# The two fp32 head loads of k, issued by SyncE and ScalarE at once, in an attention and FFN kernel bound by TensorE

## Chip, cores, metric

The kernel runs on one core of a Trainium2 chip. The metric is the device time of one execution in microseconds (us). The "span" of a profile runs from the first to the last instruction of the program; the time is some 1.8 us longer than the span.

## The reference

Cross-covariance attention (channels attend to channels) in four batches, then a maxout FFN with three up-projections.

```python
# q, k, v: (4, 6144, 256) float32
qn = q / (norm(q, axis=1) + 1e-6);  kn = k / (norm(k, axis=1) + 1e-6)
s  = kn.transpose(0, 2, 1) @ qn / tau            # (4, 256, 256)
a  = softmax(s, axis=-1)
x  = (v @ a).reshape(4 * 6144, 256)
h  = maximum(maximum(x @ w1, x @ w2), x @ w3)    # d_ff = 768
out = h @ w_out
```

## The kernel before

Before any FFN work can start, the whole of q and k of batch 0 must be read and their Gram matrix formed. POOL loads both with a cast from float32 to fp8 on the way (the software queue). Only the first 8 of k's 48 row groups, the "head", come as float32 through SyncE's hardware queue, in two halves, and are cast on VectorE and ScalarE, so that TensorE can start early.

```python
HEAD = 8
kf = consts.tile([P, HEAD, C], FP32, name="kf")
HH = HEAD // 2
for i in range(2):
    SP.dma_start(out=kf[:, i * HH:(i + 1) * HH, :], in_=k_r[0][:, i * HH:(i + 1) * HH, :])
for load, widths in ((load_k, [8] * 5), (load_q, [8] * 5 + [4, 2, 2])):   # POOL, fp32 -> fp8
    ...
DVE.tensor_copy(out=qk[0][1][:, 0:HH, :], in_=kf[:, 0:HH, :], saturate=False)
ACT.activation(out=qk[0][1][:, HH:HEAD, :], in_=kf[:, HH:HEAD, :], func=AF.Copy, saturate=False)
...
def gram(b):
    for tp in range(NG // 2):          # 24 pairs of row groups: squares of k, 2 matmuls each
        ... PE.matmul(kk[:, jsl], lhsT=kt[:, tsl, jsl], rhs=kt[:, tsl, jsl], ...)
    ... dkm = kk * ident               # VectorE
    for tp in range(NG // 2):          # 24 pairs: q against k, and squares of q, 4 matmuls each
        ... PE.matmul(ps[j][:, 0:C], lhsT=qt[:, tsl, jsl], rhs=kt[:, tsl, :], ...)
        ... PE.matmul(ps[j][:, C:C + P], lhsT=qt[:, tsl, jsl], rhs=qt[:, tsl, jsl], ...)
```

The q loads have widths 8, 8, 8, 8, 8, 4, 2, 2, so the fifth full load feeds pairs 16 to 19 of the second loop and the last small one feeds pair 23 alone.

Of the kernel before, what the change touches and what calls it, by code (L numbers as in the profile page):

```python
# [31 lines left out]
def kernel(  # L32
# [15 lines left out]
    ACT = nc.scalar  # L48
    POOL = nc.gpsimd
    SP = nc.sync  # L50
# [15 lines left out]
    k_r = k.rearrange("b (p g) c -> b p g c", p=P)  # L66
# [48 lines left out]
    HEAD = 8  # L115
    kf = consts.tile([P, HEAD, C], FP32, name="kf")
    HH = HEAD // 2
    for i in range(2):
        SP.dma_start(out=kf[:, i * HH:(i + 1) * HH, :], in_=k_r[0][:, i * HH:(i + 1) * HH, :])
    for load, widths in ((load_k, [8] * 5), (load_q, [8] * 5 + [4, 2, 2])):  # L120
        g0 = HEAD if load is load_k else 0
        for w in widths:
# [358 lines left out]
```

## Time and profile before

| | kernel before |
|---|---|
| time, median of the first 3 runs | 576.76 us |
| span of the profile | 574.9 us |
| kf halves have landed (their casts start) | 4.68 and 5.93 us |
| fifth full q load lands | 31.27 us |
| last q load lands | 33.44 us (18.43 us issue + 15.0 us) |

The page's list of DMA issues shows what is loaded in the head: columns are destination and source, issuing queue, count, KB each (as written), and the median us from issue to landing.

```profile
k_sb<-in_k_dram POOLq DMA_DIRECT2D x5, 256.0 KB, 10.8
q_sb<-in_q_dram POOLq DMA_DIRECT2D x5, 256.0 KB, 19.4
kf<-in_k_dram SPq DMA_DIRECT2D x2, 512.0 KB, 4.3
```

A time to landing of 10 or 19 us for 256 KB says that these loads stand in a queue. The issue is early, the DMA engines are the limit.

### The profile page before, as it was taken

How to read it: one execution, taken by the hardware profiler on the slowest of the kernel's cores; microseconds unless marked ns; L12 is line 12 of the kernel's file. 1: busy time of each engine (PE TensorE's matmuls, PEld its weight loads, DVE VectorE, ACT ScalarE, POOL GpSimd, SP SyncE). 2: the span in 40 equal slices, each digit the busy share in tenths (PEclk: the TensorE clock that was granted, in tenths of full speed). 3: DMA queues.
4: the chain of work that ended last, by engine and by line, in shares of the span. 5: the costliest groups of instructions: out<-in, count | busy, mean ns of one | idle time of the engine just before them, and what ended most of it. 6: DMA issues, size and time to landing. Idle time of an engine off the chain costs nothing.

```text
span 574.9 us, 9325 instructions
## 1 busy us (share of the span) xinstructions
PE 555.1 (97%) x3328; PEld 328.5 (57%) x3328; DVE 406.4 (71%) x627; ACT 307.2 (53%) x530; POOL 227.3 (40%) x235
## 2 busy tenths in 40 slices
PE   3789999999999999999999999999999999999996
PEld 3655555555755555555575555555575555555554
DVE  0048777777577777777748777777848778778774
ACT  1034567677454466776735447767646444444442
POOL 4232257776731028777761006777760000000000
PEclk9999999999999999999999999999999999999999
DMA  9998998885598228977378526788535234322111
GB/s 142 107 144 157 130 178 124 157 133 113 102 118 164 59 66 155 133 152 130 75 131 130 114 75 101 157 131 130 125 84 127 66 82 129 74 91 76 56 73 74
DMA packets 75951, 65.62 MB, mean 114 GB/s; under 512 B 52353, under 2 KB 61953, under 8 KB 75905
## 3 DMA queue, kind: packets, MB, share of 16 engines
q0 software_dynamic: 18928, 26.48, 39.1%
q1 hardware_dynamic: 56832, 38.28, 22.9%
q8 instruction: 26, 0.43, 0.3%
q10 hardware_dynamic: 144, 0.26, 0.1%
q14 instruction: 21, 0.16, 0.1%
HBM read 78.64 MB, written 25.17 MB: 181 GB/s over the span
## 4 chain that ended last, share of the span: by engine, by line
PE 93%; DMA 5%; ACT 0%; DVE 0%; issue 0%; POOL 0%; DVEq 0%; POOLq 0%
PE h_ps L327 65%; PE o_ps L346 21%; DMA q_sb<-in_q_dram 4%; PE gram L235 3%; PE ew_ps L282 3%; DMA k_sb<-in_k_dram 2%; PE o_ps L366 0%; PE gram L178 0%; PE n_ps L216 0%; PE n_ps L218 0%; ACT et L246 0%; PE gram L180 0%; DVE o_sb L372 0%; POOL k_sb L99 0%; DVE scr L253 0%
## 5 line engine op out<-in xcount | busy, mean ns | idle before, releaser
L327 PE MATMUL h_ps<-vt_sb,aw_sb 128*128 128x512 bf16 x1728 | 406.6, 379 | 0.0
L331 DVE TENSOR_TENSOR s_mx<-h_ps,s_mx 128x512 bf16<-128x512 f32 x288 | 197.9, 687 | 98.1 <-ACT s_mx L330 97.1
L327 PEld LDWEIGHTS <-aw_sb 128*128 128x128 bf16 x1728 | 168.2, 98 | 163.0 <-DVE aw_sb L288 3.7
L330 ACT ACTIVATE s_mx<-h_ps 128x512 bf16<-128x512 f32 x288 | 171.4, 595 | 130.7 <-PE h_ps L327 130.7
L332 DVE TENSOR_TENSOR ht_sb<-h_ps,s_mx 128x512 bf16<-128x512 f32 x288 | 199.2, 692 | 30.7 <-PE o_ps L346 0.5
L204 POOL TENSOR_TENSOR acc<-acc,sq 128x768 f32<-128x768 f32 x90 | 147.7, 1651 | 70.7 <-ACT sq L198 70.5
L346 PE MATMUL o_ps<-wo_sb,ht_sb 128*128 128x256 bf16 x1128 | 153.9, 273 | 0.0
L346 PEld LDWEIGHTS <-ht_sb 128*128 128x128 bf16 x1128 | 110.4, 98 | 52.9
L349 ACT ACTIVATE o_sb<-o_ps 128x512 f32<-128x512 f32 x94 | 56.1, 597 | 83.1 <-PE o_ps L346 83.1
L110 POOL DMA_DIRECT2D v_sb<-in_v_dram x48 | 26.8, 562 | 88.5 <-DMA vt_sb<-v_sb 86.6
L198 ACT ACTIVATE sq<-q_sb 128x768 bf16<-128x768 fp8e4 x48 | 40.5, 844 | 0.0
L198 ACT ACTIVATE sq<-k_sb 128x768 bf16<-128x768 fp8e4 x48 | 40.1, 835 | 0.0
L201 POOL CAST acc<-sq 128x768 f32<-128x768 bf16 x6 | 4.9, 821 | 64.6 <-ACT sq L198 64.6
L102 POOL DMA_DIRECT2D q_sb<-in_q_dram x32 | 17.7, 555 | 10.7 <-DMA k_sb<-in_k_dram 9.7
L166 PE MATMUL kk<-k_sb 128*128 128x256 fp8e4 x48 | 7.8, 339 | 11.7 <-DVE k_sb L152 5.4
L285 ACT ACTIVATE aw_sb<-ew_ps,rinv 128x384 bf16<-128x384 f32 (+1 forms) x27 | 14.4, 546 | 5.7 <-PE ew_ps L282 4.8
L282 PE MATMUL ew_ps<-w_sb,et 128*128 128x384 bf16 (+1 forms) x108 | 17.1, 308 | 0.0
L235 PE MATMUL gram<-k_sb,q_sb 128*128 128x512 fp8e4 x144 | 16.8, 277 | 0.0
L99 POOL DMA_DIRECT2D k_sb<-in_k_dram x29 | 16.0, 554 | 1.0 <-POOLq L462 0.8
L235 PEld LDWEIGHTS <-q_sb 128*128 128x256 fp8e4 x144 | 15.9, 136 | 0.6
L178 PE MATMUL gram<-k_sb,q_sb 128*128 128x512 fp8e4 x48 | 10.7, 323 | 3.4 <-DMA q_sb<-in_q_dram 3.4
L166 PEld LDWEIGHTS <-k_sb 128*128 128x256 fp8e4 x48 | 6.5, 182 | 12.8 <-DMA k_sb<-in_k_dram 6.3
(52 smaller groups left out, 103.6 us busy)
## 6 DMA issues: line engine op xcount, KB each, us to landing
out_dram<-o_sb SPq DMA_DIRECT2D x47, 512.0 KB, 2.8
v_sb<-in_v_dram POOLq DMA_DIRECT2D x48, 256.0 KB, 3.7
k_sb<-in_k_dram POOLq DMA_DIRECT2D x24, 192.0 KB, 5.3
q_sb<-in_q_dram POOLq DMA_DIRECT2D x24, 192.0 KB, 6.8
k_sb<-in_k_dram POOLq DMA_DIRECT2D x5, 256.0 KB, 10.8
q_sb<-in_q_dram POOLq DMA_DIRECT2D x5, 256.0 KB, 19.4
w_sb<-in_moe_w_dram POOLq DMA_DIRECT2D x9, 128.0 KB, 5.7
kf<-in_k_dram SPq DMA_DIRECT2D x2, 512.0 KB, 4.3
```

The lines of the kernel that those rows point to most:

```text
L102: POOL.dma_start(out=qk[b][0][:, g0:g0 + w, :], in_=q_r[b][:, g0:g0 + w, :])
L110: POOL.dma_start(out=t, in_=v_r[gi // NCH, gi % NCH])
L198: ACT.activation(out=sq, in_=src, func=AF.Square)
L204: POOL.tensor_tensor(out=acc, in0=acc, in1=sq, op=ALU.add)
L235: PE.matmul(g[:, j * C:(j + 1) * C], lhsT=qt[:, tsl, j * P:(j + 1) * P], rhs=kt[:, tsl, :], start=(tp == 0 and j == 0), stop=(tp == NG // ...
L282: PE.matmul(ew[:, :w], lhsT=et[:, j, ic * P:(ic + 1) * P], rhs=w_sb[m][:, j, fsl], start=(j == 0), stop=(j == CC - 1))
L327: PE.matmul(t.rearrange("p (t n) -> p t n", t=TPC), lhsT=aw[m][:, ic, fsl], rhs=vt[:, :, ic, :], start=(ic == 0), stop=(ic == CC - 1))
L330: ACT.activation(out=s_mx, in_=hp[0], func=AF.Copy)
L331: DVE.tensor_tensor(out=s_mx, in0=hp[1], in1=s_mx, op=ALU.max)
L332: DVE.tensor_tensor(out=ht[:, fc, :], in0=hp[2], in1=s_mx, op=ALU.max)
L346: PE.matmul(st["ps"][:, half], lhsT=ht[:, fc, t * P:(t + 1) * P], rhs=wo_sb[:, fc, :], start=(fc == 0), stop=(fc == FC - 1))
L349: ACT.activation(out=st["o"][:, t - 1:t + 1, :].rearrange("p t d -> p (t d)"), in_=st["ps"], func=AF.Copy)
```

## The change

The intent: SyncE needs 0.4 us to issue each half, so the second half is issued late. With ScalarE issuing the second one, both start together.

```diff
-    for i in range(2):
-        SP.dma_start(out=kf[:, i * HH:(i + 1) * HH, :], in_=k_r[0][:, i * HH:(i + 1) * HH, :])
+    for i, eng in enumerate((SP, ACT)):
+        eng.dma_start(out=kf[:, i * HH:(i + 1) * HH, :], in_=k_r[0][:, i * HH:(i + 1) * HH, :])
```

## The prediction

> **What bounds the kernel now.** I read the page first, for the balance of the engines and the chain that ended last, and then the first 60 us of the chain in order of time, because the diff touches only the first 6 us.
>
> ```profile
> span 574.9 us, 9325 instructions
> PE 555.1 (97%) x3328; PEld 328.5 (57%) x3328; DVE 406.4 (71%) x627; ACT 307.2 (53%) x530; POOL 227.3 (40%) x235
> ...
> PE 93%; DMA 5%; ACT 0%; DVE 0%; issue 0%; POOL 0%; DVEq 0%; POOLq 0%
> ```
>
> The reader is to see that TensorE carries 93% of the chain and DMA 5%. A head load can touch only that 5%, which is 29 us. The chain in order of time says which 29 us:
>
> ```profile
> 1.23 0.67 POOL k_sb L99
> 1.90 8.89 DMA k_sb<-in_k_dram
> 10.79 0.28 issue
> 11.07 20.20 DMA q_sb<-in_q_dram
> 31.27 0.04 issue
> 31.32 0.32 PE gram L178
> ```
>
> Start, duration, piece. The chain goes through the software-queue loads (those that POOL issues, float32 to fp8) until 31.27 us, and from there through TensorE to the end. The two kf loads and the two casts out of kf are not in it by name. So the time of this kernel is, to a good approximation, "when the last q load lands" plus 543.6 us of TensorE work that the change does not touch. The question is whether the kf loads decide when the last q load lands. For that I read the instructions of the first 8 us in order of time:
>
> ```profile
> 0.73 1.28 ACT L144 ACT_TABLE_LOAD   x1 [0.73 <-PEq L462]
> 0.74 0.87 SPq L119 DMA_DIRECT2D kf<-in_k_dram  x2
> 1.23 2.79 POOL L99 DMA_DIRECT2D k_sb<-in_k_dram  x5 [0.78 <-POOLq L462]
> 4.68 0.69 DVE L152 CAST k_sb<-kf 128x1024 fp8e4<-128x1024 f32 x1 [3.40 <-DMA kf<-in_k_dram]
> 5.93 1.06 ACT L153 ACTIVATE k_sb<-kf 128x1024 fp8e4<-128x1024 f32 x1 [3.91 <-DMA kf<-in_k_dram]
> 8.35 1.07 PEld L166 LDWEIGHTS <-k_sb 128*128 128x256 fp8e4 x8 [0.75 <-DMA k_sb<-in_k_dram]
> 8.35 1.25 PE L166 MATMUL kk<-k_sb 128*128 128x256 fp8e4 x8 [0.57 <-DMA k_sb<-in_k_dram]
> ```
>
> SyncE issues both kf loads in 0.87 us, the second at about 1.15 us. The halves land at 4.68 and 5.93 us. TensorE has done both halves by 7.8 us and then waits for the first software load at 8.35 us. Last, the stretches, with the columns window, length, busy time of PE, PEld, DVE, ACT and POOL, granted clock, DMA share, GB/s:
>
> ```profile
> 1.50:2.00 0.50, 0.00 (x0) 0.00 (x0) 0.00 (x0) 0.50 (x1) 0.50 (x2) 1.00 0.78 106
> 2.00:2.50 0.50, 0.00 (x0) 0.00 (x0) 0.00 (x0) 0.02 (x1) 0.50 (x2) 1.00 0.73 123
> 2.50:3.00 0.50, 0.00 (x0) 0.00 (x0) 0.00 (x0) 0.00 (x0) 0.50 (x2) 1.00 0.81 213
> 3.50:4.00 0.50, 0.00 (x0) 0.00 (x0) 0.00 (x0) 0.00 (x0) 0.50 (x2) 1.00 1.07 434
> 12.00:14.00 2.00, 0.82 (x7) 0.74 (x6) 0.00 (x0) 0.00 (x0) 0.49 (x1) 1.00 1.07 108
> ```
>
> The DMA engines are busy from 1.75 us (first packet of kf in the packet records) without a gap. The rate is counted in bytes written, so the 108 GB/s of the fp8 stage reads four times as much, 432 GB/s, the same as the 434 of the kf stage at its best. The one weak stretch is 1.75 to 3.0 us, where the engines are "busy" at 0.73 to 0.81 but move only 106 to 213 GB/s: the first packets take 0.2 to 1.2 us each instead of the 0.159 us of the later ones. Two queue rows (packets, MB, share), up to 3.00 us and up to 4.75 us, finish the picture:
>
> ```profile
> q1 hardware_dynamic: 54, 0.22, 38.8%
> ...
> q1 hardware_dynamic: 243, 0.93, 60.8%
> q0 software_dynamic: 1, 0.00, 0.4%
> ```
>
> The software queue (q0), whose first load was issued by 1.90 us, moves its first packet only at 4.74 us, when kf (q1) is nearly drained. In the packet records each DMA engine starts its first software packet some 6 ns after its own last kf packet, between 4.74 and 5.5 us. So kf holds the software loads back, and through them it is on the path after all: whatever makes kf drain sooner moves the last q load and the whole span by the same amount.
>
> **What the skill says.** The Trainium skill, page "DMA: Bandwidth & Descriptors", section "Issuing engines are not separate DMA queues", says that loads started from several engines run on the same 16 DMA engines and that doing so "will only save the time on the sequencer it takes to initiate the DMA". Here that time is about 0.4 us (0.87 us for two issues). The same page, section "Where 436 GB/s comes from", puts the ceiling of the fabric at 435 GB/s; this trace agrees with 432 to 434, so there is no spare rate for a second issuer. Its section "Queues, rings and completion order" has each DMA engine go round its queues packet by packet. The trace of before does not look like that between the hardware and the software queue (no software packet before 4.74 us), so I don't count on fair sharing. The page "ScalarE: Activation LUTs", section "What ACT_TABLE_LOAD costs", gives a load of 1283 ns; the trace shows 1.28 us.
>
> **The change part by part.** The comparison of instruction streams shows one DMA issue leaving SyncE and one arriving on ScalarE, ahead of its table load. TensorE, VectorE and POOL keep their order; the two casts wait on swapped semaphores and on nothing new.
>
> SyncE loses one issue, 0.41 us. Its next instruction is a transpose at 42 us, so that is worth nothing.
>
> ScalarE gains one issue of about 0.4 us (its final output issue in this trace takes 0.37 us). The table load moves from 0.73 to about 1.15 us and ends near 2.4 us. ScalarE then waits for kf until 5.93 us, so 3.5 us of slack remain. Cost 0.
>
> The second kf half is issued at 0.74 instead of 1.15 us, 0.41 us sooner. What is this worth? Its packets could reach the DMA engines one latency after the issue: for the first half 1.75 - 0.74 = 1.01 us, so at 2.16 us before and at 1.75 after. But at 2.16 us the engines still have the first half to do: 128 packets, of which 54 had begun by 3.00 us. So the second half is queued in time in both kernels and the 0.41 us lie fully beside busy DMA engines. By this step the gain is 0.
>
> What can move is the slow start. From 1.75 to 3.00 us 54 packets began; at 0.159 us on 16 engines it would have been 1.25 x 16 / 0.159 = 126. The 72 missing packets are 72 x 0.159 / 16 = 0.72 us of engine time. If two rings let an engine have two slow first packets in flight, half may be saved, 0.36 us; if an engine serves one packet at a time, nothing is. I weigh the first at one third: 0.12 us.
>
> The halves will now share the engines and land close together, near 5.3 to 5.9 us. The VectorE cast moves from 4.68 to perhaps 5.4 us, and the ScalarE cast is earlier or the same. TensorE needs 2 x 0.75 us for both halves and would be done at about 7.8 us or before, still ahead of 8.35 us. Cost 0, and even 1 us of delay would be absorbed: between later k loads it idles some 1.2 us each.
>
> Sum: 0 - 0 - 0.12, rounded to -0.15 us: 576.76 - 0.15 = 576.6 us.
>
> **The rivals.** First, the issue time is on the path and the whole 0.41 us comes back, giving 576.35. For it: the chain starts with an issue, and software loads wait for kf. Against it: the DMA engines are busy all the time between the two issues. Second, the slow start is cut by parallel rings, 0.36 to 0.72 us, giving 576.0 to 576.4. For it: busy 0.75 and low rate mean that latency and not rate limits there. Against it: the slow packets look like a cold start of the memory path[...]. Third, a loss: SyncE's and ScalarE's rings mix at the start, the first half lands later, or three rings disturb the order of the software loads, and TensorE is late at one of its waits; +0.1 to +0.4 us, 576.9 to 577.2. For it: the VectorE cast surely moves later. Against it: the slack of about 1.2 us before each k load. Fourth, the software loads get in earlier between the kf packets: bytes are conserved at 432 GB/s, so the last q load lands at the same time, 576.76.
>
> **Range and chances.** Rivals one and two reach down to about 576.0, the third up to 577.1, and the three runs of before agree to 0.01 us. So 576.6, range 576.0 to 577.1. Two per cent is 11.5 us; the kf loads as a whole take 2.4 us at full rate (1.05 MB / 434 GB/s). No rival comes near. Faster 0.01, same 0.98, slower 0.01.
>
> **What would show it.** In the changed profile: a ScalarE issue at about 0.74 us and the table load after it; both casts starting within 0.5 us of one another; the first software packet at 4.4 to 4.9 us; the last q load landing at 30.6 to 31.4 us in place of 31.27; the rest shifted with it unchanged. A hardware queue's rate in 1.5 to 3.0 us well above 106 to 213 GB/s would speak for the second rival. The prediction is wrong if the last q load moves by more than 0.7 us, or if the span moves and that landing does not, for then TensorE's later stages have changed.

## The result, and the profile after

The changed kernel took 577.14 us (median of 6 runs, 577.0 to 578.7), the kernel before 576.80 in the same session (576.76 to 576.92). The ratio is 1.001 with an interval of 0.9997 to 1.0023. Ratios here are the mean time of one kernel's fast runs over the mean of the other's in the same rounds, so not quite the ratio of the medians. "Same" at 2% was right. The range, 576.0 to 577.1, was missed by 0.04 us, and the small gain that was expected is a small loss.

First the head of the changed kernel, six lines picked from its instructions in order of time (start, us, engine, instruction, idle time before and what ended it).

```profile
0.73 0.39 ACTq L119 DMA_DIRECT2D kf<-in_k_dram  x1
0.74 0.40 SPq L119 DMA_DIRECT2D kf<-in_k_dram  x1
1.16 1.28 ACT L144 ACT_TABLE_LOAD   x1 [1.16 <-PEq L462]
5.64 1.06 ACT L153 ACTIVATE k_sb<-kf 128x1024 fp8e4<-128x1024 f32 x1 [3.20 <-DMA kf<-in_k_dram]
5.80 0.69 DVE L152 CAST k_sb<-kf 128x1024 fp8e4<-128x1024 f32 x1 [4.51 <-DMA kf<-in_k_dram]
8.27 1.26 PE L166 MATMUL kk<-k_sb 128*128 128x256 fp8e4 x8 [0.47 <-DMA k_sb<-in_k_dram]
```

The issues do start together. The halves land together too, so the VectorE cast moved from 4.68 to 5.80 us and the ScalarE cast from 5.93 to 5.64. TensorE still waits for the first software load, at 8.27 instead of 8.35 us. Next the slow start of the DMA engines, the same stretches as in the prediction, and the queue rows up to 3.00 us (packets, MB, share).

```profile
1.50:2.00 0.50, 0.00 (x0) 0.00 (x0) 0.00 (x0) 0.50 (x1) 0.50 (x2) 1.00 0.93 90
2.00:2.50 0.50, 0.00 (x0) 0.00 (x0) 0.00 (x0) 0.44 (x1) 0.50 (x2) 1.00 0.50 98
2.50:3.00 0.50, 0.00 (x0) 0.00 (x0) 0.00 (x0) 0.00 (x0) 0.50 (x2) 1.00 0.78 254
```

```profile
q10 hardware_dynamic: 38, 0.16, 29.8%
q1 hardware_dynamic: 16, 0.07, 7.0%
```

Queue q10 is ScalarE's, q1 SyncE's. Together 38 + 16 = 54 packets had begun by 3.00 us, exactly as many as with one queue. That they are equal to the packet is chance: over the traces it was 51 to 63 with both issues on SyncE (8 traces, mean 55) and 53 to 63 with one on each (7 traces, mean 57), and two packets are 0.02 us of 16 engines' time. The first software packet starts at 4.76 us (4.74 before), and by 31 us the software queue has finished 2.743 MB (2.741 before; both from the packet records). So no time was won at the start.

Where does the loss arise? The chain that ended last, in order of time, from the changed kernel and then from the kernel before (start, us, piece):

```profile
10.95 20.25 DMA q_sb<-in_q_dram
31.20 0.05 issue
31.25 0.32 PE gram L178
...
33.75 0.06 PE gram L180
33.80 0.04 issue
33.85 0.32 PE gram L178
```

```profile
33.65 0.06 PE gram L180
33.70 0.11 PE gram L178
33.82 0.06 PE gram L180
33.87 0.11 PE gram L178
```

At 31.25 us the changed kernel is still 0.07 us ahead. At 33.6 us TensorE stands still in front of pair 23, the one that reads the last small q load, and takes it up at 33.85; the kernel before came to it at 33.71 and went on without a stop. The rows for that last load, before and then after:

```profile
q_sb<-in_q_dram POOLq DMA_DIRECT2D x1, 64.0 KB, 15.0
```

```profile
q_sb<-in_q_dram POOLq DMA_DIRECT2D x1, 64.0 KB, 15.5
```

Issued at 18.43 and 18.34 us, it landed at 33.44 and 33.80 us. The same bytes had moved, the fifth full load was 0.07 us earlier, and yet the last one was 0.36 us later. The traces hold 16 completions for each load, one for the share of each DMA engine, and the load has landed with the last of them. So I took the 16 completions of a load apart (worked out from the landing records of the traces; us after the first completion, in order).

```
before, 4th full q load (27.29): 0 .04 .05 .11 .13 .16 .19 .20 .34 .34 .40 .43 .47 .48 .49  .67
before, last q load     (32.30): 0 .05 .05 .13 .17 .20 .22 .34 .34 .41 .43 .47 .49 .50 .69 1.14
after,  4th full q load (27.26): 0 .06 .06 .16 .24 .25 .26 .27 .33 .34 .39 .45 .47 .48 .51  .62
after,  last q load     (32.27): 0 .06 .07 .16 .24 .26 .27 .27 .33 .33 .39 .47 .49 .52 .64 1.54
```

Fifteen of the sixteen keep their places, within 0.1 us, from the first software load at 8 us to the last. One falls back by about 1 us between 27 and 31 us: in the kernel before the one that stood at about .14 is gone and 1.14 is new, after the change the one at about .47 is gone and 1.54 is new. Between the two there is one other event on the DMA engines, in the queue rows from 28.9 to 30.4 us of both kernels:

```profile
q8 instruction: 1, 0.02, 4.1%
```

It is an instruction fetch, one packet of 16 KB that takes 0.97 us (in the packet records at 29.27 us before, 29.00 after). This gives Theory A: the fetch falls on one DMA engine and makes it a straggler by 1 us. The queue never runs empty, so about 1 us of delay stays to the last load (a part can be made up: in `pe_early_after` below the spread is 1.61 us at the fourth q load, 1.05 at the fifth and 1.08 at the last), and when the last q load lands depends on where that engine happened to stand in the line of sixteen.

A second part lies behind the span. The profiled run before took 576.67 us, of which 1.79 are behind the span of 574.88; the changed one 577.14, of which 2.09 behind 575.05.

### The profile page after: what moved, and what is told of

The parts are those of the page before. It is cut to its first block, busy times and chain, and to the rows that moved or that the text cites. A ratio compares the mean times of both kernels' runs of the same rounds, so it can differ in the third digit from the quotient of the medians.

```text
span 575.1 us, 9324 instructions
## 1 busy us (share of the span) xinstructions
PE 555.2 (97%) x3327; PEld 328.6 (57%) x3328; DVE 406.5 (71%) x627; ACT 307.0 (53%) x530; POOL 227.1 (39%) x235
## 4 chain that ended last, share of the span: by engine, by line
PE 93%; DMA 5%; ACT 0%; issue 0%; DVE 0%; POOL 0%; DVEq 0%; POOLq 0%
PE h_ps L327 65%; PE o_ps L346 21%; DMA q_sb<-in_q_dram 4%; PE gram L235 3%; PE ew_ps L282 3%; DMA k_sb<-in_k_dram 2%; PE o_ps L366 0%; PE gram L178 0%; PE n_ps L216 0%; PE n_ps L218 0%; ACT et L246 0%; PE gram L180 0%; DVE o_sb L372 0%; POOL k_sb L99 0%; DVE scr L253 0%
## 5 line engine op out<-in xcount | busy, mean ns | idle before, releaser
L110 POOL DMA_DIRECT2D v_sb<-in_v_dram x48 | 26.8, 562 | 89.0 <-DMA vt_sb<-v_sb 87.1
L282 PEld LDWEIGHTS <-et 128*128 128x128 bf16 x108 | 10.5, 98 | 5.6
```

The lines of the kernel that those rows point to most:

```text
L110: POOL.dma_start(out=t, in_=v_r[gi // NCH, gi % NCH])
L282: PE.matmul(ew[:, :w], lhsT=et[:, j, ic * P:(ic + 1) * P], rhs=w_sb[m][:, j, fsl], start=(j == 0), stop=(j == CC - 1))
```

## The experiments

Theory A is the straggler. Its rivals: B, the landing is noise of one session and not a matter of the kernel; C, the ScalarE issue as such costs the time; D, the straggler is a slow DMA engine and the fetch a coincidence; and for the part behind the span F and G, the number of SyncE's or of ScalarE's instructions. E says that the change costs time inside the span, because the first half lands later.

"Mean" is that of the fast runs below 577.5 us. In eight of the kernels, the one before among them, one or two runs came out at 577.8 to 578.7 us, a mode of its own that the section on the runs' surprises explains; the official intervals contain it.

### Does it repeat, and is it the issuers? (again, swap, both_act, one_sp)

`again` is the changed kernel as it is.

> The changed kernel as it is, a second time, to see whether its loss of 0.2 to 0.4 us is a property of the kernel or of one session. Theory A (one DMA engine is a straggler: a 16 KB instruction fetch of about 1 us falls on it at 29 us, and how late the last q load lands depends on where that engine stood in the line before; the two kf issues have put it 0.35 us later in the line): the engines' order is reproducible, so again 577.0 to 577.2 against 576.8, last q load landing at 33.8 us with a spread of its 16 completions of 1.5 us. Rival B (the landing is noise of one session): spread and landing anywhere between 33.3 and 33.9, time on either side of 576.8.

```diff
 # swap
-    for i, eng in enumerate((SP, ACT)):
+    for i, eng in enumerate((ACT, SP)):
```

> The two issuers exchanged: ScalarE issues the first half, SyncE the second. Theory A: the first packets are shared out among the engines in another way, so the straggler may stand anywhere: last q load landing between 33.3 and 33.9 us, and the in-span time moves by exactly the landing minus 33.7 us where it is later than that (TensorE's own arrival), by at most -0.1 us where it is earlier. Rival C (the ScalarE issue itself costs the time, e.g. through the later table load): the same +0.2 us in the span as the changed kernel whatever the landing, 577.1.

```diff
 # both_act
-    for i, eng in enumerate((SP, ACT)):
+    for i, eng in enumerate((ACT, ACT)):
```

> Both halves issued by ScalarE, one after the other, SyncE none: a single ring as in the kernel before, but the table load about 0.8 us later. Theory A: one ring in order gives the engines the stagger of the kernel before, last q load near 33.4 us, span 574.8 to 575.0 and time 576.7 to 576.9. Rival C: the loss of 0.2 to 0.4 us stays or doubles, 577.1 to 577.5, with the landing at 33.4.

```diff
 # one_sp
-    for i in range(2):
-        SP.dma_start(out=kf[:, i * HH:(i + 1) * HH, :], ...)
+    SP.dma_start(out=kf, in_=k_r[0][:, 0:HEAD, :])
```

> One SyncE issue of 1 MB in place of two of 512 KB: no second issue at all. If the issue time mattered, this is at least as good as the change: 576.4. Theory A: the DMA engines are full from the first packet on, so the bytes moved by 31 us are the same within 10 KB; the two casts both wait for about 5.9 us, without cost; the time follows the last q load alone, 576.7 to 577.2.

Measured, beside 576.75 us for the kernel before (median of 9): again 576.87, swap 577.09, both_act 576.71, one_sp 576.93; all four intervals of the ratio contain 1. By these numbers nothing can be told apart, but the traces of the profiled runs can. TensorE's path through the gram stage has two gates. From its start on the fifth q load to the exponential that follows the gram stage it needs 4.01 us, and from the landing of the last q load 1.72 us (both read from the traces in which that gate closes later). The later of the two should give the start of the exponential, and the rest of the span is 539.5 to 539.6 us:

| profile | start on 5th load | last load lands | later gate | exponential starts | span |
|---|---|---|---|---|---|
| before | 31.32 | 33.44 | 35.33 (5th) | 35.33 | 574.88 |
| after | 31.25 | 33.80 | 35.52 (last) | 35.52 | 575.05 |
| again | 31.47 | 33.59 | 35.48 (5th) | 35.48 | 574.99 |
| swap | 31.23 | 33.67 | 35.39 (last) | 35.38 | 574.89 |
| both_act | 31.24 | 33.66 | 35.38 (last) | 35.37 | 574.88 |
| one_sp | 31.09 | 33.46 | 35.18 (last) | 35.17 | 574.79 |

The rule holds to 0.01 us. Its two constants are read from these same traces, so a test needs others: in the nine later traces without a dip of the clock it gives the start of the exponential within 0.02 us. All six have one straggler: the spread of the last load's 16 completions is 1.14, 1.54, 1.44, 1.45, 1.43 and 1.32 us. But `again` is the changed kernel, and its landing is 33.59 instead of 33.80: the place of the straggler is not a property of the kernel. My expectation that the order of the engines is reproducible is wrong, and Rival B is right about that part. `both_act`, with one issuing queue as in the kernel before, landed at 33.66 and not at 33.4 as expected, for the same reason. `one_sp` shows once more that the issue time is worth nothing: with no second issue at all its mean is no faster. One of its expectations was missed: by 31 us its software queue had finished 2.762 MB, 21 KB more than the kernel before and not the same within 10 KB.

### Is the fetch the cause? (sq_before, sq_after, pe_early, pe_early_after, sq_again)

The Trainium skill, page "Runtime: NRT & Kernel Launch", section "Instruction fetch mechanics", says that an engine's instructions are refilled in blocks of 16 KiB, 256 instructions, by DMA, and that crossing a block boundary is "mostly hidden". The size agrees with the packet of 16 KB. If the fetch is TensorE's, it must move when TensorE has fewer or more instructions ahead of it. `sq_before` takes 72 away: for 36 of k's 48 row groups the squares go to ScalarE and their sum to VectorE, both idle here.

```diff
-        for tp in range(NG // 2):
+        acc = sm.tile([P, SQW * C], FP32, name="acc_h")
+        for g0 in range(0, 36, SQW):
+            sq = sq_pool.tile([P, SQW * C], BF16, name="sq")
+            ACT.activation(out=sq, in_=kt[:, g0:g0 + SQW, :]..., func=AF.Square)
+            ... DVE: acc = sq, later acc += sq
+        for tp in range(36 // 2, NG // 2):
 ...
+        for i in range(SQW):
+            DVE.tensor_tensor(out=dkm, in0=dkm, in1=acc[:, i * C:(i + 1) * C], op=ALU.add)
```

> The kernel before with 36 of the 48 row groups of k normed on ScalarE (square) and VectorE (sum), both idle in the head, in place of TensorE: 72 TensorE instructions fewer ahead of the gram stage, the result still correct. Theory A: the 16 KB instruction fetch follows TensorE's place in its program (in six traces it comes within 0.05 us of the start of the same matmul, at 29.0 to 29.4 us), so it moves behind the last q load, past 32.6 us; no straggler, the fifth full q load lands near 30.4 instead of 31.2 to 31.4, the last near 33.0 instead of 33.4 to 33.8, and the span gets 0.6 to 0.9 us shorter: 575.9 to 576.2. Rival D (the straggler is a slow DMA engine as such, the fetch a coincidence): landings and time as before, 576.75.

`sq_after` is the same edit on the changed kernel.

> The same with the two kf issues on SyncE and ScalarE. Theory A: without a straggler the issue split has nothing left to act on, so this agrees with sq_before within 0.1 us, 575.9 to 576.2, or is better by up to 0.1. Rival C or E (the split itself costs 0.1 to 0.3 us, by its ScalarE issue or by a later first half): the difference of the first pair stays, sq_after slower than sq_before by 0.1 to 0.35 us. ScalarE now starts squaring right after the cast, so a late cast of ScalarE or VectorE would also show here, but behind 12 us of slack.

`pe_early` adds 32 TensorE instructions instead, while TensorE waits for the first data; `pe_early_after` does so in the changed kernel.

```diff
+        dm = htile("dm")
+        for i in range(16):
+            PE.matmul(dm[:, :P], lhsT=warm[:, :P], rhs=warm[:, :P], start=(i == 0), stop=(i == 15))
         kk = htile("kk")
```

> The kernel before with 16 small matmuls on a zero tile ahead of the first k tile, while TensorE waits anyway: 32 more TensorE instructions, so by Theory A the fetch comes some 4 pairs of row groups earlier, near 26.5 to 27 us, and since the DMA queue never runs empty the straggler stays one for the rest: fourth full q load at 28.6 to 28.9 instead of 27.96 us, fifth and last as before (31.2 to 31.4 and 33.4 to 33.8), time 576.6 to 577.0. Rival D: fourth load at 27.96 as before.

> The changed kernel with the same 16 small matmuls. Theory A: as pe_early, with its own place of the straggler: last q load 33.4 to 33.8 us, time 576.7 to 577.2, the difference from pe_early between -0.1 and +0.3 us. It serves as one more pair for whether the split costs anything at all.

`sq_again` is `sq_before` once more, in another session.

> The kernel without the straggler a second time, since 2 of its 6 executions (and 1 of 5 of its sister) were slow, at 584 to 600 us with a granted clock of 0.98 to 0.997. If these belong to the kernel, one or two of five are slow again; if they were the session, none. Fast runs 575.9 to 576.3 either way, no completion of the q loads later than 0.7 us behind the first.

The chain of `sq_before` in order of time, and the row of its last q load:

```profile
10.98 19.38 DMA q_sb<-in_q_dram
30.36 0.04 issue
30.40 0.32 PE gram L189
...
32.96 0.26 PE gram L189
33.22 0.07 PE gram L191
```

```profile
q_sb<-in_q_dram POOLq DMA_DIRECT2D x1, 64.0 KB, 14.6
```

The fifth load lands at 30.36 instead of 31.27 us, the last at 32.85. Its 16 completions lie within 0.64 us: there is no straggler. The fetch comes at 33.88 us, behind the last q load. The exponential starts at 34.56 us (32.85 + 1.72 = 34.57), 0.77 us before that of the kernel before, and the span is 574.1 us. Means: sq_before 576.03, sq_after 576.22, sq_again 576.18 us, against 576.75 and 576.68 for the kernel before. The spans of the fast runs below 577.5 are 574.0 to 574.4 in all three, those of the kernel before 574.7 to 575.3: they do not overlap. (Nine of the ten runs of the kernel before beside sq_before are those of the batch before it on the same chip; sq_again has eleven of its own session.) The official intervals (0.9973 to 1.0004 for sq_before) still include 1, so the gain of 0.1% rests on the spans and the mechanism.

In `pe_early` the fetch is at 26.75 us, in the queue rows of 26 to 28 us:

```profile
q0 software_dynamic: 117, 0.21, 104.2%
q8 instruction: 1, 0.02, 2.8%
```

The straggler comes earlier with it, as expected: the fourth q load lands at 28.83 us with a spread of 1.50 us (27.96 and 0.67 before, when the fetch came after that load). TensorE reaches pair 12 at 28.87 us (28.01 before), pair 16 at 31.09 and pair 23 at 33.67, by the last load's landing at 33.62. The span is 574.9 us, the mean 576.57; pe_early_after has 576.67 with the last load at 33.34; these three are just below what was expected (576.6, 576.7 and 33.4). So an earlier straggler is still one at the last load. In sixteen of the seventeen traces, 224 to 231 TensorE instructions had begun when the fetch started, wherever it fell in time between 26.8 and 34.2 us (so the same place in the program to a few matmuls, not to the 0.05 us that the expectation of sq_before names). Only pe_early has 208; its TensorE still ran at half pace until 26.7 us (25.3 us in pe_early_after), but whether that is the reason is open. So the fetch is TensorE's, and Rival D, a coincidence, is out. That the same DMA engine takes it each time is not shown: the packet records don't name the engine.

What of the change itself? With the straggler gone, sq_after has a mean span of 574.12 us against 574.17 in sq_before, so inside the span the change costs nothing. Its time is 0.19 us longer all the same, behind the span: 2.09 against 1.86 us (1.97 without one run of 2.48). With pe_early it is 574.66 against 574.73 us in the span, and 2.01 against 1.84 us behind it.

`sq_before` and its kind are not a version to keep as they are: 4 of 17 executions came out slow (585, 587, 585 and 600 us, granted clock 0.982 to 0.997), one of them in the repeat in another session. Of 36 timed executions of the kernel before in these sessions, none did. Why is open.

### What lies behind the span? (again2, after_spx, before_actx, before_act1, before_act2, before_spx)

In eleven of the first fourteen traces the time minus the span equals the end of the last 8 KB instruction fetch behind the program, less 0.24 us (after: 2.33 and 2.09; both_act: 2.39 and 2.16; sq_after: 2.14 and 1.89). Where that fetch ends sooner, as in the kernel before (1.95 and 1.79), something else limits. So the question is what delays it: from 1.61 us behind the span before to 1.80 after. `again2` is the changed kernel a third time.

> The changed kernel a third time, beside the next two. Until now the time beyond the profiled span (time minus span, of each run) was 1.74 to 1.95 us (mean 1.84) in the kernel before and 1.84 to 2.15 (means 1.93 and 2.05) in the changed one, and in the traces the last instruction fetch of 8 KB after the program's end starts 1.59 to 1.63 us behind the span in three kernels with two kf issues on SyncE, 1.78 to 2.00 in those with one or none. Theory F (part of the loss, 0.1 to 0.2 us, lies behind the span and hangs on SyncE's number of instructions): time minus span 1.9 to 2.1 again, in-span difference within 0.15 us of zero with either sign, as the straggler falls.

```diff
 # after_spx, on the changed kernel; before_spx the same on the kernel before; before_actx with ACT
+            if gi == 5:
+                spare = consts.tile([16, C], FP32, name="spare")
+                SP.dma_start(out=spare, in_=k_r[0][0:16, 0, :])
```

> The changed kernel with one small extra SyncE load (16 KB, unused) in the sixth chunk, so that SyncE issues as many instructions as before. Theory F: time minus span back to 1.75 to 1.95 (mean near 1.84), last fetch near 1.6 us behind the span, time about 0.15 us below again2, unless its straggler differs. Rival C (the ScalarE issue as such): time minus span stays at 1.9 to 2.1.

> The kernel before with the same extra load issued by ScalarE: one more ScalarE instruction, SyncE's two kf issues kept. Theory F: time minus span 1.75 to 1.95 as before. Rival C: 1.9 to 2.1.

```diff
 # before_act1 (n = 1), before_act2 (n = 2)
+    scrap = consts.tile([P, 1], BF16, name="scrap")
+    for _ in range(n):
+        ACT.activation(out=scrap, in_=ones_c, func=AF.Copy)
```

> The kernel before with one tiny unused ScalarE copy in the head: one more ScalarE instruction, no DMA moved. Theory G (time behind the span follows the number of instructions of an engine, through the start of the last fetch): last fetch starts 1.75 to 1.95 us behind the span in place of 1.6, time minus span 1.9 to 2.1. Rival C (the ScalarE DMA issue as such): fetch at 1.6, time minus span 1.75 to 1.95. In the span nothing but the straggler's scatter, 574.7 to 575.1.

> The same with two copies. Theory G: as with one or later, up to 2.0 us for the fetch (the kernel with both kf issues on ScalarE had 1.94). Rival C: 1.6 us and 1.75 to 1.95.

> The kernel before with one small extra SyncE load in the sixth chunk: one more SyncE instruction, ScalarE unchanged. If SyncE's number counts, the fetch moves away from 1.6 us behind the span, in either direction; if only ScalarE's does (Theory G narrowed) or only its DMA issue (Rival C), it stays at 1.6 and time minus span at 1.75 to 1.95.

| kernel | mean time | mean span | mean behind the span | last fetch starts, us behind the span of the profiled run |
|---|---|---|---|---|
| before (the three sessions after the first) | 576.68 to 576.75 | 574.84 to 574.91 | 1.82 to 1.86 | 1.61 |
| after / again / again2 | 577.10 / 576.87 / 576.89 | 575.04 / 574.94 / 574.90 | 2.06 / 1.93 / 1.99 | 1.80 / 1.78 / slow run |
| swap | 577.02 | 575.05 | 1.97 | 1.79 |
| both_act | 576.75 | 574.76 | 1.99 | 1.94 |
| one_sp | 576.88 | 574.95 | 1.93 | 1.78 |
| after_spx | 576.97 | 574.98 | 1.99 | 1.73 |
| before_actx | 576.73 | 574.80 | 1.93 | 1.91 |
| before_spx | 576.66 | 574.73 | 1.93 | 1.65 |
| before_act1, before_act2 | 576.77, 576.81 | 574.92, 574.95 | 1.84, 1.86 | 1.61, 1.62 |
| pe_early, sq_before | 576.57, 576.03 | 574.73, 574.17 | 1.84, 1.86 | 1.63, 1.59 |

(The one execution of again2 that was profiled fell in a very slow state, 742.8 us at a granted clock of 0.76; it is left out. One run of sq_again had 2.91 us behind its span; its other four fast runs have 1.84 in the mean.) Theory F, SyncE's number of instructions, falls: after_spx restores it and stays at 1.99. Theory G, ScalarE's number, falls with before_act1 and before_act2, at 1.84 and 1.86. Rival C, the ScalarE DMA issue as such, fits these two, but one_sp and before_spx have no early ScalarE issue and still 1.93. What fits every row is weaker: the kernels whose DMA issues on the hardware queues are those of the kernel before, in number and issuer, have 1.82 to 1.86 us behind the span, and all others have 1.93 to 2.09. This grouping was found afterwards, and no run was made to test it. By what way an issue of a DMA, in the head or in the sixth chunk, would shift a fetch after the end is open.

## Why the prediction was right and wrong

- **"By this step the gain is 0"** for the 0.41 us of issue time: right. The engines were full, and one_sp without a second issue gained nothing either.
- **The slow start, -0.12 us**: the term was mis-sized, it measured 0. Packets begun by 3.00 us are 54 and 54, the first software packet starts at 4.74 and 4.76 us, bytes by 31 us agree within 2 KB. What makes the first packets slow, a "cold start of the memory path" or something else, no run tested.
- **Casts and TensorE ahead of 8.35 us, cost 0**: right. The VectorE cast was later than thought (5.80, not 5.4 us), TensorE had done both halves by 7.81 us. The prediction's 1.15 us for SyncE's second issue is 1.20 in the trace, so 0.46 us and not 0.41 were hidden; nothing hangs on it.
- **"When the last q load lands plus 543.6 us of TensorE work that the change does not touch"**: this step failed. 31.27 us is the landing of the fifth full load. Two small loads follow, the last landed at 33.44 us, 0.27 us before TensorE came to it at 33.71. That was all the margin. After the change the small load landed at 33.80, TensorE waited for it until 33.85, and this wait, not the one at 31.25, ended last. The check that the prediction gave, the landing at 30.6 to 31.4 us, came true (31.20) while the span moved the other way, which by its own words meant that a later stage had changed.
- **"The three runs of before agree to 0.01 us"**, and so the lower and upper ends: wrong as a measure of scatter. Later sessions of the kernel before ran from 576.45 to 577.13 us (one more at 577.85), and with the straggler in another place the last load landed at 33.80, 33.59 and 33.81 us in three traces of the changed kernel.
- **The third rival, "three rings disturb the order of the software loads", +0.1 to +0.4 us** had the size and the wrong place: it is a wait at a q load, not at a k load, and the order of the loads did not change.
- **What no step had**: the time behind the span. Between the two profiled runs the time grew by 0.47 us: 0.17 in the span, by that wait, and 0.30 behind it; in the means of the later sessions 0.09 and 0.17 behind it. Its cause stays open.
- **"Some 6 ns after its own last kf packet"**: a wrong reading. The packet records don't name the engine; what they show is in the section on what was not expected.
- **"This trace agrees with 432 to 434"**: the 432 GB/s are an estimate of what is read, four times the 108 GB/s written. Only the 434 GB/s of the kf stage are a rate into SBUF, which the 435 GB/s of the cited section count.

In all, three sessions give +0.28, +0.12 and +0.21 us for the change by their means (577.10 - 576.82, 576.87 - 576.75, 576.89 - 576.68). Each official interval contains 1. In the two sessions with spans of both kernels, +0.03 and +0.04 lie in the span and +0.09 and +0.17 behind it. That the first session fell outside the range is this small loss together with one unlucky place of the straggler, not time lost in the head.

## What to carry to other kernels

Before you hide the issue of a DMA, check in the packet or queue rows whether the DMA engines would have idled in that time; if they have work, the gain is nothing. A load is as late as the last of its 16 shares, and in a queue that never runs empty most of a delay of one engine stays until the end, so look for single late completions, and for which load each wait belongs to by tile and size rather than by a chain that merges them. Differences of 0.05% need the scatter of several sessions, not three equal runs.

## What the runs showed of the hardware that was not expected

- No packet of the software queue starts before 4.74 us in the kernel before, although its first load had been issued by 1.90 us; by then 243 of the 288 kf packets had begun. Of its first 40 packets 14 start exactly 2 ns after the end of a kf packet, in both kernels (at most 7 at any other distance up to 60 ns; worked out from the packet records). This looks as if each DMA engine turned to the software queue when its kf packets were done. It is argued, since the records don't name the engine, and whether the software queue had its packets ready earlier is not shown.
- The runs at 577.8 to 578.7 us show a granted clock of 0.995 to 0.997, the other fast runs of these kernels 0.998 to 1.0. One of them was profiled, in before_act1, and there it is a change of clock in the gram stage; stretches, with the granted clock third from the end:

```profile
28.00:31.00 3.00, 1.43 (x16) 1.26 (x16) 0.00 (x0) 0.34 (x1) 0.70 (x1) 1.00 1.06 106
...
32.00:33.00 1.00, 1.00 (x10) 1.00 (x8) 0.00 (x0) 0.00 (x0) 0.91 (x2) 0.53 1.16 183
...
34.00:35.00 1.00, 1.00 (x9) 1.00 (x8) 0.00 (x0) 0.00 (x0) 0.49 (x2) 0.50 1.43 192
...
36.00:37.00 1.00, 1.00 (x6) 0.41 (x6) 0.86 (x6) 0.45 (x3) 0.94 (x2) 1.00 1.44 193
```

  TensorE waits about 2 us for the fifth q load, and shortly after it the clock is at half until about 35.5 us; the exponential started at 36.96 us instead of 35.3 to 35.5. The wait that the straggler lengthens (1.98 us between matmul starts before, 1.18 in sq_before) may thus also be a risk of a throttled clock. That is argued, not shown: before_act1 waited 2.11 us, but both_act and one_sp waited 2.14 and 2.15 us without a dip.

## What the Trainium skill lacked or had wrong

- "Runtime: NRT & Kernel Launch", section "Instruction fetch mechanics", calls the cost of a block boundary mostly hidden. Here one fetch of 16 KB (0.97 us) put one DMA engine 1 us behind in a full queue, and moving it behind the loads shortened the span by about 0.75 us (574.9 to 574.1).
- "DMA: Bandwidth & Descriptors", section "Queues, rings and completion order", has each DMA engine take its queues in turn, packet by packet, where it has work for them. It gives no help with the start of the software queue here: 0 software packets until 4.74 us, 2.8 us after its first load was issued, while 243 kf packets began. Whether the queue had no work ready or was passed over, no run shows.
- No page says what sets the start of the last instruction fetch after the program's end. It came 1.61 us behind the span before and 1.80 after the change, with 0.09 to 0.30 us more time; that the DMA issues cause this is not shown.
